# A decode step's output in two column halves, with filler products on TensorE

## The chip, the cores and the metric

The kernel runs on one core of a Trainium2 chip. The core has TensorE (matrix products, PE in the profile), VectorE (DVE), ScalarE (ACT), GpSimd (POOL) and SyncE (SP); SP and ACT issue the transfers here, and 16 transfer engines carry them out. The metric is the time of one execution on the device in microseconds (us), as the median of several runs.

## The reference

One decode step for two sequences (B = 2, one token each, D = 448): layernorm, attention of 16 query heads on 8 cached key and value heads (head size 256), limited to the last 2048 of 8192 cached positions, an output projection, and a gate from a small two-layer branch.

```python
W = min(4096, max(256, Sk // 4))                      # 2048
q = (xn @ wq)                                         # 2 x 16 heads x 256
scores = einsum(q, k[:, :, Sk - W:]) * Dh ** -0.5
o = softmax(scores) @ v[:, :, Sk - W:]
s = o.reshape(B, 1, 4096) @ wo                        # 2 x 448
g = silu(relu(xn @ w1) @ w2)                          # 2 x 448
return x + s * g                                      # bfloat16
```

All inputs are bfloat16. The keys and values inside the window are 2 x 16.8 MB; with the weights the kernel reads 44 MB and writes 1.8 KB.

## The kernel before

Every instruction is recorded by hand into one list for each engine (`pr.op`, `pr.dma`) with what it depends on; each engine runs its list in the order written, and waits on semaphores only where a dependence was given. There is no scheduler: the order of the Python code is the order on each engine. All products are recorded by the helper `mm`, so in the profile they all have its line (L246) and are told apart by their tiles.

The work goes in four units `u` (two sequences by two groups of four key heads). Each unit has one large buffer `kv[u]` of 128 partitions: first it holds K, later V. SP's queue carries nearly all the loads in this order: wq, w1, w2, K0 to K3, then V0, V1, V2 and the two halves of V3 (each V waits until the scores of its unit are done, as it overwrites K), then wo in six pieces of 16, 4, 4, 4, 2 and 2 rows a partition (`WO_PARTS`). ACT's queue loads x twice, as `x_sb` (two rows, for the layernorm) and as `x_c` (spread out for the last addition).

The order around the change:

- `do_H`, `do_F`: the gate's branch, early on. `do_F` brings the sum of four partial results to the layout of the output with a small float32 selection matrix (`bsel`), and makes silu with ACT's exponential and three VectorE steps, giving `g_sb`.
- For each unit: VectorE turns K (`do_turn`), TensorE makes scores (`do_S`), VectorE and ACT the softmax (`do_max`, `do_et`), and after the last one its results are spread into the weights `pt` (`do_spread`, `do_pt`).
- `do_PV(u)`: 32 products of 512 columns, in four column tiles of TensorE that run side by side, into the bank `obk`. For the last unit the second 16 wait for the second half of V3 (`d_vb`). `do_out(u)`: two VectorE steps take the result to `o_sb` (the buffer `xg`). `do_turn_out(hg)`: eight products and a VectorE copy (L368) turn it into `at2`, the weights of the output projection.
- The output projection: for the first 16 rows of wo (`WO_TILED`) 16 products of 448 columns into `wbk`, four side by side, copied by VectorE to `wc` (L448). The other 16 rows go straight into `fbk` (`direct`): for each row four products of 112 columns, one in each column tile, so that a quarter of the output's columns comes out in each group of 32 partitions. `at2` has 32 columns a row of wo, of which columns 0 and 16 hold the two sequences and the others zeros. Between rows 19 and 20 `wc` is added into `fbk` with `bsel`.
- The end: `fbk` times `g_sb` (L468), plus `x_c` (L470), over 128 partitions of 112 columns; then two stores, one for each sequence: SP stores the first, ACT the second, each as four rows of 112 values that lie 32 partitions apart.

Of the kernel before, what the change touches and what calls it, by code (L numbers as in the profile page):

```python
# [74 lines left out]
def bass_recurrent_scan__sliding_block_cached__dense_activation_relu__decode_kernel(  # L75
# [11 lines left out]
    B, Sq, D = A_x.shape  # L87
    _, HKV, SK, DH = A_k_cache.shape
# [10 lines left out]
    SLOTS = 7  # L99
    HC = HD // 2  # L100
    FC = DFF // 2
    NCOL = D // 4
    WO_PARTS = [16, 4, 4, 4, 2, 2]
    WO_TILED = 16

    es = contextlib.ExitStack()
    with es:
        pr = _Prog(nc, es)

        def named(name, shape, dt):  # L110
            return es.enter_context(nc.sbuf_tensor(name, shape, dt))
# [17 lines left out]
        bsel = named("bsel", [128, 32], F32)  # L129
# [45 lines left out]
        def rows(t):  # L175
            w = t.shape[1]
            return bass.AP(t, 0, [[16 * w, 8], [1, w]])

        def kv_src(u, cache):
            b, hg = divmod(u, 2)  # L180
            return cache[b, 4 * hg:4 * hg + 4, SK - W:SK, :].rearrange("g (p t) d -> p g (t d)", t=NT)

        d_x = pr.dma(ACTE, x_sb[0:B, :], A_x[:, 0, :])
        p_xc = pr.op(POOL, lambda e: e.memset(x_c[:, :], 0.0))
        d_xc = pr.dma(ACTE, rows(x_c), A_x.rearrange("b s (i n) -> i (b s) n", i=4), [p_xc])
        wq_src = A_wq.rearrange("r (hf c) -> (r hf) c", hf=2).rearrange("(p s) c -> p (s c)", s=SLOTS)
        w1_src = B_w1.rearrange("r (hf c) -> (r hf) c", hf=2).rearrange("(p s) c -> p (s c)", s=SLOTS)
        w2_src = B_w2.rearrange("(p j) n -> p (j n)", j=14)
# [7 lines left out]
        for u in range(NU):  # L196
# [4 lines left out]
            out=ident[:, :], in_=ident[:, :], compare_op=ALU.not_equal, fill=1.0,  # L201
            base=0, pattern=[[-1, 128]], channel_multiplier=1), [i0])
        p_z = [pr.op(POOL, lambda e, t=t: e.memset(t[:, :], 0.0))
               for t in (asel, bsel, rm, bt, qstat, at2)][-1]

        v_bn = pr.op(DVE, lambda e: e.bn_stats(st6[0:B, :], x_sb[0:B, :]), [d_x])
        v_ag = pr.op(DVE, lambda e: e.bn_aggr(st2[0:B, :], st6[0:B, :]), [v_bn])
# [7 lines left out]
        def z(t):  # L215
            return a_z[t.name]
# [17 lines left out]
        v_bs = pr.op(DVE, lambda e: e.tensor_copy(view(bsel, 0, [[16, 2]]), f8[:, 0:2]), [v_f8, p_z])  # L234
# [10 lines left out]
        def mm(out_ap, lhsT, rhs, start, stop=False, **kw):  # L245
            return lambda e: e.matmul(out_ap, lhsT=lhsT, rhs=rhs, start=start, stop=stop,  # L246
                                      skip_group_check=True, **kw)
# [83 lines left out]
        def do_rs():  # L331
# [2 lines left out]
                out=view(rs, 0, [[2, NU], [1, 2]]), in0=view(half2, 0, [[0, NU], [1, 2]]),  # L334
                in1=view(rinv, 0, [[1, NU], [0, 2]]), op=ALU.mult), [v, v_h2])

        def do_PV(u):
            bank, p, v = obk, pt[u], kv[u]
            deps = [d_v[u], st["pt", u], z(bank), st.get(("osb", u - 1))]
            for n in range(NT // 2):  # L340
                i = n % 4
                if u == NU - 1 and n == NT // 4:
                    deps = [d_vb]
                o = pr.op(PE, mm(bank[32 * i:32 * i + 16, :], p[:, 16 * n:16 * n + 16],
                                 v[:, 2 * n * DH:2 * n * DH + 2 * DH],
                                 n < 4, n >= NT // 2 - 4, tile_position=(0, 32 * i)), deps)
                deps = []
            last_PV[u] = o
# [9 lines left out]
                op0=ALU.mult, op1=ALU.add), [v])  # L358

        def do_turn_out(hg):  # L360
            deps = [st["osb", 2 + hg], v_as, st["mbk"]]
            lo = 64 * hg
            for dq in range(8):
                o = pr.op(PE, mm(mbk[lo:lo + 64, 288:352], asel[:, 7 - dq:71 - dq],
                                 view(o_sb, hg * 2 * DH + 32 * dq, [[DH, B], [1, 32]]),
                                 dq == 0, dq == 7, tile_position=(0, lo)), deps)
                deps = []
            st["at"] = st["mbk"] = pr.op(DVE, lambda e: e.tensor_copy(  # L368
                view(at2, 0, [[16, B], [32, 32]], n=64, p0=lo), view(mbk, 288, [[32, B], [1, 32]], n=64, p0=lo)), [o, p_z])

        def do_H():
            deps = [st["w1"], v_xr, v_q]
# [12 lines left out]
        def do_F():  # L385
            deps = [st["w2"], st["h"], z(fbk)]
            for j in range(14):
                i = j % 4
                o = pr.op(PE, mm(fbk[32 * i:32 * i + B, 0:D], h_sb[:, 32 * j:32 * j + 2], w2_sb[:, j * D:j * D + D],
                                 j < 4, j >= 10, tile_position=(0, 32 * i)), deps)  # L390
                deps = []
            v = pr.op(DVE, lambda e: e.tensor_copy(zc[:, :], fbk[:, 0:D]), [o])
            deps = [v, v_bs, st["mbk"]]
# [4 lines left out]
            a_e = pr.op(ACTE, lambda e: e.activation(ea[:, :], mbk[:, 128:128 + NCOL], ACT.Exp, scale=-1.0), [o])  # L398
            v = pr.op(DVE, lambda e: e.tensor_scalar(
                out=ea[:, :], in0=ea[:, :], scalar1=1.0, scalar2=None, op0=ALU.add), [a_e])  # L400
            v = pr.op(DVE, lambda e: e.reciprocal(tmp[:, :], ea[:, :]), [v])
            st["g"] = st["mbk"] = pr.op(DVE, lambda e: e.tensor_tensor(
                out=g_sb[:, :], in0=mbk[:, 128:128 + NCOL], in1=tmp[:, :], op=ALU.mult), [v])
# [35 lines left out]
        for n in WO_PARTS:  # L439
            landed[j0] = pr.dma(SP, wqo[:, j0 * D:(j0 + n) * D], wo_src[:, j0 * D:(j0 + n) * D], [m_q])  # L440
            j0 += n
        deps = [st["at"], z(wbk)]
        for j in range(WO_TILED):
            i = j % 4
            o = pr.op(PE, mm(wbk[32 * i:32 * i + B, 0:D], view(at2, 32 * j, [[16, 2]]), wqo[:, j * D:j * D + D],
                             j < 4, j >= WO_TILED - 4, tile_position=(0, 32 * i)), deps + [landed.get(j)])
            deps = []
        v_wc = pr.op(DVE, lambda e: e.tensor_copy(wc[:, :], wbk[:, 0:D]), [o])  # L448
# [19 lines left out]
        v_t = pr.op(DVE, lambda e: e.tensor_tensor(  # L468
            out=tmp[:, :], in0=fbk[:, 0:NCOL], in1=g_sb[:, :], op=ALU.mult), [m_o, st["g"]])
        v_o = pr.op(DVE, lambda e: e.tensor_tensor(  # L470
            out=out_sb[:, :], in0=tmp[:, :], in1=x_c[:, :], op=ALU.add), [v_t, d_xc])
# [34 lines left out]
```

## Time and profile before

| | |
|---|---|
| median of 3 runs | 111.02 us (110.95 to 111.13) |
| the profiled execution | 110.76 us, of which the span from the first to the last instruction is 109.4 us |
| busy, share of the span | PE 51%, DVE 56%, ACT 8%, POOL 3% |
| read from memory | 44.11 MB, 403 GB/s over the span |
| chain that ended last, by engine | DMA 57%, DVE 28%, PE 7%, SP's queue 5% |
| mean granted TensorE clock | 0.875 |

A row of a timeline or of the groups names line, engine, operation, output tile and input tiles, shape and count; in square brackets or behind the last bar stands how long the engine was idle before it and what ended that. A share of the granted clock of 1.00 is TensorE's full speed, 0.50 half of it. In the row of a stretch each engine has its busy time and, in parentheses, its instructions.

### The profile page before, as it was taken

Reading aid. Unit: us, or ns where it says so; the run is one execution under the profiler, and the core shown is the slowest. Engines: PE = TensorE matmul, PEld = TensorE weight load, DVE = VectorE, ACT = ScalarE, POOL = GpSimd, SP = SyncE. Lnnn points to the kernel's source line nnn. Section 1 sums busy time; section 2 is a strip of 40 time slices with the busy share of each in tenths; the row PEclk is TensorE's granted clock in tenths of the full one; section 3 lists DMA queues with packets and bytes.
Section 4 is the critical chain, followed back from the end, with each engine's and each line's share of the span. In section 5 each row is a group of like instructions: output and inputs, shape, how many; then the busy total and the mean of one; then the engine's idle time right before and its main releaser. Section 6 shows DMA issues by size and latency. Waiting matters only on the chain.

```text
span 109.4 us, 1124 instructions
## 1 busy us (share of the span) xinstructions
PE 55.5 (51%) x479; PEld 15.0 (14%) x479; DVE 61.6 (56%) x84; ACT 9.0 (8%) x18; POOL 2.9 (3%) x13
## 2 busy tenths in 40 slices
PE   0010649450000079929943994499349555425780
PEld 0000204110000011001200120111033122201350
DVE  2920046424099979999999999920457333103122
ACT  2970000000000000002000200020110000000000
POOL 7300000000000000000000000000000000000000
PEclk9999999999999999985996799589955899955559
DMA  6898999999999989998999899999999999999940
GB/s 158 356 472 365 426 436 494 395 479 449 395 395 479 467 383 395 491 455 383 407 494 431 383 419 503 419 395 413 503 407 395 413 431 431 425 421 405 400 170 1
DMA packets 2628, 44.17 MB, mean 404 GB/s; under 512 B 318, under 2 KB 576, under 8 KB 960
## 3 DMA queue, kind: packets, MB, share of 16 engines
q1 hardware_dynamic: 2600, 44.11, 94.6%
q8 instruction: 3, 0.05, 0.2%
q10 hardware_dynamic: 24, 0.00, 0.0%
q14 instruction: 1, 0.01, 0.0%
HBM read 44.11 MB, written 0.00 MB: 403 GB/s over the span
## 4 chain that ended last, share of the span: by engine, by line
DMA 57%; DVE 28%; PE 7%; SPq 5%; issue 1%
DMA kv<-in_A_k_cache_dram 34%; DVE kv L281 24%; DMA wqo<-in_A_wo_dram 23%; PE sbk L246 7%; SPq L35 5%; DVE q_x L310 1%; DVE rm L298 1%; DVE rm_t L300 0%; DVE bias L304 0%; DVE bt L301 0%; PE fbk L246 0%; DVE tmp L468 0%; DVE out_sb L470 0%
## 5 line engine op out<-in xcount | busy, mean ns | idle before, releaser
L246 PE MATMUL sbk<-kv,qstat 128*8 128x512 bf16 x128 | 30.0, 1085 | 23.3 <-DVE kv L281 23.3
L281 DVE STREAM_TRANSPOSE kv<-kv 128x2048 f32<-128x2048 f32 x16 | 35.6, 2274 | 4.9 <-DMA kv<-in_A_k_cache_dram 4.9
L246 PE MATMUL obk<-kv,pt 128*16 128x512 bf16 x128 | 10.3, 472 | 6.3 <-DMA kv<-in_A_v_cache_dram 3.6
L246 PEld LDWEIGHTS sbk<-kv,qstat 128*8 128x8 bf16 x128 | 4.8, 107 | 47.1 <-DVE kv L281 29.5
L353 DVE TENSOR_SCALAR o_odd<-obk,rs 128x256 f32<-128x256 f32 x4 | 1.9, 484 | 11.9 <-PE obk L246 11.9
L305 ACT ACTIVATE e_sb<-sbk,bias 128x512 bf16<-128x512 f32 x4 | 2.8, 689 | 52.1 <-DVE bias L304 52.1
L246 PE MATMUL qbk<-wqo,xr 128*4 128x512 bf16 x28 | 3.2, 626 | 5.4 <-DMA wqo<-in_A_wq_dram 5.4
L264 DVE TENSOR_SCALAR q_x<-qbk 128x512 bf16<-128x512 f32 x1 | 0.7, 691 | 8.4 <-PE qbk L246 8.4
L298 DVE TENSOR_REDUCE rm<-sbk 128x1 f32<-128x512 f32 x4 | 2.6, 662 | 4.8 <-PE sbk L246 4.8
L246 PEld LDWEIGHTS obk<-kv,pt 128*16 128x16 bf16 x128 | 3.4, 101 | 12.0 <-issue 6.4
L310 DVE STREAM_TRANSPOSE q_x<-e_sb 128x512 bf16<-128x512 bf16 x4 | 2.8, 690 | 1.7 <-ACT e_sb L305 1.7
L246 PE MATMUL mbk<-ident,xg 2*128 2x2 bf16 x7 | 0.3, 163 | 6.1 <-DVE xg L239 6.1
L327 DVE TENSOR_TENSOR pt<-spk,pmask 128x512 bf16<-128x512 f32 x4 | 2.6, 683 | 0.8 <-PE spk L246 0.8
L246 PE MATMUL qbk<-w_sb,xr 128*2 128x448 bf16 x28 | 2.8, 572 | 0.0
L246 PE MATMUL fbk<-w_sb,h_sb 128*2 128x448 bf16 x14 | 1.7, 566 | 1.5 <-issue 1.5
L246 PE MATMUL fbk<-wqo,at 128*32 128x112 bf16 x64 | 2.1, 287 | 0.2 <-DMA wqo<-in_A_wo_dram 0.2
L246 PE MATMUL spk<-q_x,perm 128*32 128x128 bf16 x16 | 0.6, 296 | 3.1 <-DVE q_x L310 3.1
L246 PE MATMUL mbk<-xg,asel 128*64 128x64 bf16 x16 | 1.1, 221 | 2.2 <-DVE xg L356 2.2
L275 DVE CAST qstat<-mbk 32x256 bf16<-32x256 f32 x4 | 1.7, 421 | 0.7 <-PE mbk L246 0.7
L246 PE MATMUL wbk<-wqo,at 128*2 128x448 bf16 x16 | 1.7, 567 | 0.7 <-DMA wqo<-in_A_wo_dram 0.7
L356 DVE SCALAR_TENSOR_TENSOR xg<-obk,rs,o_odd 128x256 bf16<-128x256 f32 x4 | 1.9, 484 | 0.1
L246 PEld LDWEIGHTS fbk<-wqo,at 128*32 128x32 bf16 x64 | 1.6, 133 | 1.0 <-DMA wqo<-in_A_wo_dram 0.8
(70 smaller groups left out, 31.9 us busy)
## 6 DMA issues: line engine op xcount, KB each, us to landing
kv<-in_A_k_cache_dram SPq DMA_DIRECT2D x4, 4096.0 KB, 41.2
kv<-in_A_v_cache_dram SPq DMA_DIRECT2D x3, 4096.0 KB, 22.1
kv<-in_A_v_cache_dram SPq DMA_DIRECT2D x2, 2048.0 KB, 17.6
wqo<-in_A_wq_dram SPq DMA_DIRECT2D x1, 3584.0 KB, 11.1
w_sb<-in_B_w_dram SPq DMA_DIRECT2D x2, 1568.0 KB, 16.0
wqo<-in_A_wo_dram SPq DMA_DIRECT2D x1, 1792.0 KB, 23.4
wqo<-in_A_wo_dram SPq DMA_DIRECT2D x3, 448.0 KB, 24.4
wqo<-in_A_wo_dram SPq DMA_DIRECT2D x2, 224.0 KB, 25.1
```

Of the source, the lines that this page charges most:

```text
L35: o = _Op(eng, lambda e: e.dma_start(dst, src), [d for d in deps if d is not None], True)
L246: return lambda e: e.matmul(out_ap, lhsT=lhsT, rhs=rhs, start=start, stop=stop, skip_group_check=True, **kw)
L264: v_q = pr.op(DVE, lambda e: e.tensor_scalar(out=view(q_x, 0, [[256, 8], [128, 2], [1, 32]]), in0=view(qbk, 0, [[64, 8], [1, 2], [2, 32]]) ...
L275: st["q"] = st["mbk"] = pr.op(DVE, lambda e, Q=Q: e.tensor_copy(qstat[32 * Q:32 * Q + 32, 256 * Q:256 * Q + 256], mbk[32 * Q:32 * Q + 32, ...
L281: st["turn", u] = pr.op(DVE, lambda e, n=n: e.transpose(kf[:, 2048 * n:2048 * n + 2048], kf[:, 2048 * n:2048 * n + 2048]), [d_k[u]])
L298: v = pr.op(DVE, lambda e: e.tensor_reduce(out=rm[:, 0:1], in_=sbk[u % 2][:, :], axis=AX.X, op=ALU.max), [last_S[u], p_z, st.get(("rmt", u ...
L305: st["exp", u] = pr.op(ACTE, lambda e: e.activation(e_sb[:, :], sbk[u % 2][:, :], ACT.Exp, bias=bias[:, 0:1], accum_out=ssum[:, u:u + 1]), ...
L310: st["et", u] = pr.op(DVE, lambda e: e.transpose(q_x[:, 512 * u:512 * u + 512], e_sb[:, :]), [st["exp", u], m_qt])
L327: st["pt", u] = pr.op(DVE, lambda e: e.tensor_tensor(out=view(pt[u], 0, [[8, 64], [2, 4], [1, 2]]), in0=view(spk, 128 * u, [[2, 64], [0, 4 ...
L353: v = pr.op(DVE, lambda e: e.tensor_scalar(out=o_odd[:, :], in0=obk[:, DH:2 * DH], scalar1=rs[:, 2 * u + 1:2 * u + 2], scalar2=None, op0=A ...
L356: st["osb", u] = pr.op(DVE, lambda e: e.scalar_tensor_tensor(out=o_sb[:, lo:lo + DH], in0=obk[:, 0:DH], scalar=rs[:, 2 * u:2 * u + 1], in1 ...
```

## The change

The output is laid out as two column halves of 224 in place of four quarters of 112 (`NCOL = D // 2`). Half `c` of both sequences lies in partitions 32c and 32c + 1. So `direct` and the additions with the float32 selection have two column tiles in place of four, with two weight columns in place of 32; `at2` shrinks to two columns a row of wo, `bsel` goes (the first two columns of `f8` do its work), and the element-wise steps of the gate and of the end run on 34 partitions (`ROWS`) of 224 columns. `x_c` is loaded by two transfers. At the end SP stores the first column half of both sequences and ACT the second, each as two rows of 224 values from two adjacent partitions.

Besides, `fill(n)` records n products that nobody reads: 32 weight columns of the identity times 512 columns of `kv[0]`, into the first bank of the scores. What they depend on is long done. There are 19: ten before the second half of the last `do_PV`, two before the last `do_turn_out`, four before the first product of wo, one before the addition of `wc`, one each before rows 20 and 24.

```diff
-    NCOL = D // 4
+    NCOL = D // 2
+    ROWS = 34
...
-        at2 = named("at2", [128, 32 * 32], BF)
+        at2 = named("at2", [128, 32 * 2], BF)
...
-        d_xc = pr.dma(ACTE, rows(x_c), A_x.rearrange("b s (i n) -> i (b s) n", i=4), [p_xc])
+        d_xc = [pr.dma(ACTE, x_c[32 * c:32 * c + B, :], A_x[:, 0, NCOL * c:NCOL * c + NCOL], [p_xc]) for c in range(2)]
...
+        def fill(n):
+            for _ in range(n):
+                pr.op(PE, mm(sbk[0][0:32, :], ident[:, 0:32], kv[0][:, 0:512], True, True), [st["exp", 2], d_v[0]])
+
         def do_PV(u):
...
                 if u == NU - 1 and n == NT // 4:
+                    fill(10)
                     deps = [d_vb]
...
         def do_turn_out(hg):
+            if hg:
+                fill(2)
...
-            for i in range(4):
-                o = pr.op(PE, mm(mbk[32 * i:32 * i + 32, 128:128 + NCOL], bsel[:, :],
-                                 zc[:, NCOL * i:NCOL * i + NCOL], True, True, tile_position=(0, 32 * i)), deps)
+            for c in range(2):
+                o = pr.op(PE, mm(mbk[32 * c:32 * c + B, 0:NCOL], f8[:, 0:B], zc[:, NCOL * c:NCOL * c + NCOL],
+                                 True, True, tile_position=(0, 32 * c)), deps)
...
+        fill(4)
         deps = [st["at"], z(wbk)]
...
         def direct(j, deps):
-            for i in range(4):
-                lo = j * D + i * NCOL
-                o = pr.op(PE, mm(fbk[32 * i:32 * i + 32, 0:NCOL], at2[:, 32 * j:32 * j + 32], wqo[:, lo:lo + NCOL],
-                                 j == WO_TILED, j == 31, tile_position=(0, 32 * i)), deps)
+            for c in range(2):
+                lo = j * D + c * NCOL
+                o = pr.op(PE, mm(fbk[32 * c:32 * c + B, 0:NCOL], at2[:, B * j:B * j + B], wqo[:, lo:lo + NCOL],
+                                 j == WO_TILED, j == 31, tile_position=(0, 32 * c)), deps)
...
         for j in range(WO_TILED, 20):
             direct(j, [landed.get(j), st["g"]])
+        fill(1)
         deps = [v_wc]
-        for i in range(4):
-            pr.op(PE, mm(fbk[32 * i:32 * i + 32, 0:NCOL], bsel[:, :], wc[:, NCOL * i:NCOL * i + NCOL], False,
-                         tile_position=(0, 32 * i)), deps)
+        for c in range(2):
+            pr.op(PE, mm(fbk[32 * c:32 * c + B, 0:NCOL], f8[:, 0:B], wc[:, NCOL * c:NCOL * c + NCOL], False,
+                         tile_position=(0, 32 * c)), deps)
...
         for j in range(20, 32):
+            if j in (20, 24):
+                fill(1)
             m_o = direct(j, [landed.get(j)])
...
-            out=tmp[:, :], in0=fbk[:, 0:NCOL], in1=g_sb[:, :], op=ALU.mult), [m_o, st["g"]])
+            out=tmp[0:ROWS, :], in0=fbk[0:ROWS, 0:NCOL], in1=g_sb[0:ROWS, :], op=ALU.mult), [m_o, st["g"]])
...
-        for b, eng in ((0, SP), (1, ACTE)):
-            d_o = pr.dma(eng, out[b].rearrange("s (i n) -> (s i) n", i=4),
-                         bass.AP(out_sb, 16 * b * NCOL, [[32 * NCOL, 4], [1, NCOL]]), [v_o])
+        for c, eng in ((0, SP), (1, ACTE)):
+            d_o = pr.dma(eng, out[:, 0, NCOL * c:NCOL * c + NCOL], out_sb[32 * c:32 * c + B, :], [v_o])
             pr.op(eng, None, [d_o])
```

More of the change, by code (lines that the diff above doesn't have):

```diff
@@ L203, in bass_recurrent_scan__sliding_block_cached__dense_activation_relu__decode_kernel @@
         p_z = [pr.op(POOL, lambda e, t=t: e.memset(t[:, :], 0.0))
-               for t in (asel, bsel, rm, bt, qstat, at2)][-1]
+               for t in (asel, rm, bt, qstat, at2)][-1]
         v_bn = pr.op(DVE, lambda e: e.bn_stats(st6[0:B, :], x_sb[0:B, :]), [d_x])
@@ L368, in do_turn_out @@
             st["at"] = st["mbk"] = pr.op(DVE, lambda e: e.tensor_copy(
-                view(at2, 0, [[16, B], [32, 32]], n=64, p0=lo), view(mbk, 288, [[32, B], [1, 32]], n=64, p0=lo)), [o, p_z])
+                view(at2, 0, [[1, B], [B, 32]], n=64, p0=lo), view(mbk, 288, [[32, B], [1, 32]], n=64, p0=lo)), [o, p_z])
         def do_H():
@@ L392, in do_F @@
             v = pr.op(DVE, lambda e: e.tensor_copy(zc[:, :], fbk[:, 0:D]), [o])
-            deps = [v, v_bs, st["mbk"]]
-            for i in range(4):
-                o = pr.op(PE, mm(mbk[32 * i:32 * i + 32, 128:128 + NCOL], bsel[:, :],
-                                 zc[:, NCOL * i:NCOL * i + NCOL], True, True, tile_position=(0, 32 * i)), deps)
+            deps = [v, v_f8, st["mbk"]]
+            for c in range(2):
+                o = pr.op(PE, mm(mbk[32 * c:32 * c + B, 0:NCOL], f8[:, 0:B], zc[:, NCOL * c:NCOL * c + NCOL],
+                                 True, True, tile_position=(0, 32 * c)), deps)
                 deps = []
-            a_e = pr.op(ACTE, lambda e: e.activation(ea[:, :], mbk[:, 128:128 + NCOL], ACT.Exp, scale=-1.0), [o])
+            a_e = pr.op(ACTE, lambda e: e.activation(ea[0:ROWS, :], mbk[0:ROWS, 0:NCOL], ACT.Exp, scale=-1.0), [o])
             v = pr.op(DVE, lambda e: e.tensor_scalar(
-                out=ea[:, :], in0=ea[:, :], scalar1=1.0, scalar2=None, op0=ALU.add), [a_e])
-            v = pr.op(DVE, lambda e: e.reciprocal(tmp[:, :], ea[:, :]), [v])
+                out=ea[0:ROWS, :], in0=ea[0:ROWS, :], scalar1=1.0, scalar2=None, op0=ALU.add), [a_e])
+            v = pr.op(DVE, lambda e: e.reciprocal(tmp[0:ROWS, :], ea[0:ROWS, :]), [v])
             st["g"] = st["mbk"] = pr.op(DVE, lambda e: e.tensor_tensor(
-                out=g_sb[:, :], in0=mbk[:, 128:128 + NCOL], in1=tmp[:, :], op=ALU.mult), [v])
+                out=g_sb[0:ROWS, :], in0=mbk[0:ROWS, 0:NCOL], in1=tmp[0:ROWS, :], op=ALU.mult), [v])
         def load_v(u, lo=0, hi=NT):
@@ L444, in bass_recurrent_scan__sliding_block_cached__dense_activation_relu__decode_kernel @@
             i = j % 4
-            o = pr.op(PE, mm(wbk[32 * i:32 * i + B, 0:D], view(at2, 32 * j, [[16, 2]]), wqo[:, j * D:j * D + D],
+            o = pr.op(PE, mm(wbk[32 * i:32 * i + B, 0:D], at2[:, B * j:B * j + B], wqo[:, j * D:j * D + D],
                              j < 4, j >= WO_TILED - 4, tile_position=(0, 32 * i)), deps + [landed.get(j)])
@@ L459, in bass_recurrent_scan__sliding_block_cached__dense_activation_relu__decode_kernel @@
             direct(j, [landed.get(j), st["g"]])
+        fill(1)
         deps = [v_wc]
-        for i in range(4):
-            pr.op(PE, mm(fbk[32 * i:32 * i + 32, 0:NCOL], bsel[:, :], wc[:, NCOL * i:NCOL * i + NCOL], False,
-                         tile_position=(0, 32 * i)), deps)
+        for c in range(2):
+            pr.op(PE, mm(fbk[32 * c:32 * c + B, 0:NCOL], f8[:, 0:B], wc[:, NCOL * c:NCOL * c + NCOL], False,
+                         tile_position=(0, 32 * c)), deps)
             deps = []
         for j in range(20, 32):
+            if j in (20, 24):
+                fill(1)
             m_o = direct(j, [landed.get(j)])
         v_t = pr.op(DVE, lambda e: e.tensor_tensor(
-            out=tmp[:, :], in0=fbk[:, 0:NCOL], in1=g_sb[:, :], op=ALU.mult), [m_o, st["g"]])
+            out=tmp[0:ROWS, :], in0=fbk[0:ROWS, 0:NCOL], in1=g_sb[0:ROWS, :], op=ALU.mult), [m_o, st["g"]])
         v_o = pr.op(DVE, lambda e: e.tensor_tensor(
-            out=out_sb[:, :], in0=tmp[:, :], in1=x_c[:, :], op=ALU.add), [v_t, d_xc])
-        for b, eng in ((0, SP), (1, ACTE)):
-            d_o = pr.dma(eng, out[b].rearrange("s (i n) -> (s i) n", i=4),
-                         bass.AP(out_sb, 16 * b * NCOL, [[32 * NCOL, 4], [1, NCOL]]), [v_o])
+            out=out_sb[0:ROWS, :], in0=tmp[0:ROWS, :], in1=x_c[0:ROWS, :], op=ALU.add), [v_t] + d_xc)
+        for c, eng in ((0, SP), (1, ACTE)):
+            d_o = pr.dma(eng, out[:, 0, NCOL * c:NCOL * c + NCOL], out_sb[32 * c:32 * c + B, :], [v_o])
             pr.op(eng, None, [d_o])
```

5 lines of the change are left out of this document (removed).

## The prediction

> **What bounds the kernel now.** I read the page first (transfer rows and chain), then the chain's last steps, then the timeline of each engine over the last 16 us, then the same time in stretches that end where the granted clock steps.
>
> ```profile
> span 109.4 us, 1124 instructions
> ...
> DMA  6898999999999989998999899999999999999940
> ...
> DMA 57%; DVE 28%; PE 7%; SPq 5%; issue 1%
> ```
> ```profile
> 81.31 25.14 DMA wqo<-in_A_wo_dram
> 106.44 0.04 issue
> 106.48 0.31 PE fbk L246 x8
> ```
>
> The transfer engines are nine tenths busy in almost every slice, and the chain's last long piece is the queue itself: the last sixth of wo is issued at 81.31 and lands at 106.44 because everything ahead of it has to pass first. All that comes behind it is a short tail: 109.44 - 106.44 = 3.0 us. A change behind the loads can move only that tail, unless it makes TensorE late for the landing.
>
> ```profile
> 93.35 1.04 PE L246 MATMUL obk<-kv,pt 128*16 128x512 bf16 x16
> 97.94 1.89 PE L246 MATMUL obk<-kv,pt 128*16 128x512 bf16 x16 [3.55 <-DMA kv<-in_A_v_cache_dram]
> 100.94 0.64 PE L246 MATMUL mbk<-xg,asel 128*64 128x64 bf16 x8 [1.11 <-DVE xg L356]
> 102.28 1.67 PE L246 MATMUL wbk<-wqo,at 128*2 128x448 bf16 x16 [0.70 <-DMA wqo<-in_A_wo_dram]
> 103.72 0.59 PE L246 MATMUL fbk<-wqo,at 128*32 128x112 bf16 x16
> 104.67 0.60 PE L246 MATMUL fbk<-wc,bsel 128*32 128x112 f32 x8 [0.35 <-DVE wc L448]
> 105.04 1.27 PE L246 MATMUL fbk<-wqo,at 128*32 128x112 bf16 x40
> 106.48 0.28 PE L246 MATMUL fbk<-wqo,at 128*32 128x112 bf16 x8 [0.17 <-DMA wqo<-in_A_wo_dram]
> ```
> ```profile
> 101.61 0.44 DVE L368 CAST at<-mbk 64x64 bf16<-64x64 f32 x1 [0.73 <-PE mbk L246]
> 103.99 0.62 DVE L448 COPY wc<-wbk 128x448 f32<-128x448 f32 x1 [1.94 <-PE wbk L246]
> 106.82 0.28 DVE L468 TENSOR_TENSOR tmp<-fbk,g_sb 128x112 f32<-128x112 f32 x1 [2.20 <-PE fbk L246]
> 107.13 0.28 DVE L470 TENSOR_TENSOR out_sb<-tmp,x_c 128x112 bf16<-128x112 f32 x1
> ```
> ```profile
> 107.43 0.66 SPq L35 DMA_DIRECT2D out_dram<-out_sb  x1
> 107.43 0.55 ACTq L35 DMA_DIRECT2D out_dram<-out_sb  x1
> ```
>
> The tail is 0.3 us of products, 0.6 us of two VectorE steps, and 109.44 - 107.43 = 2.0 us for the two stores. TensorE was ready only 0.17 us before the last rows of wo, so in this execution it has almost no slack to lose. And it was slow: the two halves of the last PV are the same 16 products, 1.04 us and 1.89 us. The stretches say why.
>
> ```profile
> 85.71:89.12 3.41, 1.90 (x32) 0.77 (x32) 1.27 (x3) 0.00 (x0) 0.00 (x0) 1.00 0.89 380
> 89.12:92.53 3.41, 1.90 (x32) 0.77 (x32) 1.24 (x4) 0.00 (x0) 0.00 (x0) 1.00 1.01 432
> 92.53:95.95 3.42, 1.41 (x24) 0.64 (x24) 0.82 (x2) 0.00 (x0) 0.00 (x0) 1.00 1.00 421
> 95.95:99.36 3.41, 1.42 (x16) 0.41 (x16) 0.00 (x0) 0.00 (x0) 0.00 (x0) 0.50 1.01 433
> 99.36:102.77 3.41, 1.60 (x24) 0.78 (x20) 1.41 (x3) 0.00 (x0) 0.00 (x0) 0.50 0.96 395
> 102.77:106.19 3.42, 3.06 (x80) 1.86 (x68) 0.62 (x1) 0.00 (x0) 0.00 (x0) 0.50 0.70 277
> ```
>
> Columns: busy us of PE, weight loads, DVE, ACT, POOL, then granted clock, transfer share, GB/s. Stretches with 1.90 us of PE work are followed by clock 1.00; the one with 1.41 is followed by 0.50, which lasts until the stretch with 3.06 is over. So the wait for the second half of V3 (3.55 us) halves the clock for nearly all of the output projection.
>
> [...]
>
> **The change part by part.**
>
> Price of a product: eight rounds of four 512-column products take 1.90 us at full clock, four rounds 1.04, so a round is (1.90 - 1.04) / 4 = 0.215 us and the rest (0.18) is filling and draining. At half clock four rounds take 1.89, hence about 0.43 a round. A filler is one 512-column product alone: 0.215 or 0.43 us.
>
> *Ten fillers behind the first half of V3.* TensorE stands from 94.39 (93.35 + 1.04) to 97.94. Clock there is full until 95.95, and with fillers the stretch 92.53 to 95.95 holds about 1.41 + 1.5 = 2.9 us of work, so it stays full: 10 x 0.215 = 2.15, done at 96.6. Price 0, covered by 1.4 us of waiting that is left; at half clock they would take 4.3 and end 0.7 late. PV's second half then takes 1.04, ending 98.98.
>
> *Two fillers before the last turn of o* run to 99.4 under the two VectorE steps (98.98 to about 100.0): price 0. The turn takes about 0.44 in place of 0.64.
>
> *Four fillers before wo's first 16 rows:* from 100.45 to 101.3. The copy that feeds the rows is done at 100.0 + 0.44 + 0.03 + 0.44, 100.9, but the rows themselves land only near 102.24 (the 0.70 us wait above ends there), so price 0 with 0.9 us left.
>
> *wbk* then takes 1.04 x 448/512, about 0.93 (before 1.67), ending 103.2; wc is copied by 103.9. *Direct products* have two column tiles of 224 in place of four of 112: per row twice the time at one clock, 224/512 x 0.215 = 0.094, against 0.047. Rows 16 to 19 need 0.4, the filler 0.2, the float32 product of wc doubles in length but runs at twice the clock (0.60 less drain, again about 0.4). Rows 20 to 27 need 0.75 and two fillers 0.43. From 103.9 this sums to 105.5 to 105.6, and rows 28 and 29 follow their landing. TensorE is ready for the last landing with some 0.3 us to spare. Price of fillers and half the column tiles together: 0 so long as the clock is full.
>
> *The last two rows* (behind the landing): the second begins 0.094 after the first in place of 0.07 at least, and the last product streams 0.047 longer: +0.07 us, on the path.
>
> *The two last VectorE steps* now have 34 rows of 224. Length, not rows, sets the price:
>
> ```profile
> L327 DVE TENSOR_TENSOR pt<-spk,pmask 128x512 bf16<-128x512 f32 x4 | 2.6, 683 | 0.8 <-PE spk L246 0.8
> ...
> L332 DVE RECIPROCAL rinv<-mbk 128x4 f32<-128x4 f32 x1 | 0.2, 171 | 0.0
> ```
>
> (683 - 275)/400 = 1.02 ns an element, so 275 + 114 = 389 ns each, +0.23 us for both, on the path. x_c now has two semaphores; the second wait lies beside the first step.
>
> *The stores.* Two rows of 448 B each in place of four of 224. No such store is in the trace; the nearest row is the two-row load of x at the start, on ACT's queue:
>
> ```profile
> 0.74 0.55 ACTq L35 DMA_DIRECT2D x_sb<-in_A_x_dram  x1
> ...
> 2.07 0.62 DVE L206 BATCH_NORM_STATS2 st<-x_sb 2x6 f32<-2x448 bf16 x1 [2.07 <-DMA x_sb<-in_A_x_dram]
> ...
> 11.86 3.16 PE L246 MATMUL qbk<-wqo,xr 128*4 128x512 bf16 x28 [5.43 <-DMA wqo<-in_A_wq_dram]
> ```
>
> Its user starts 1.33 us after its issue; the pair of four-row stores takes 2.0. So the gain lies between 0 and 0.65. A loss is excluded: those rows of 896 B were longer than the new ones. I take two thirds, 0.43: the row count is that of the load, but the stores still come as a pair from two engines, and SP's half took 0.66 to issue against 0.55.
>
> [...]
>
> *The start.* x_c becomes two loads: one more issue on ACT (0.55), behind it ACT's table load, square root and clears. TensorE waits 5.43 us for wq there, so nothing comes of it. Without that cover it would cost 0.55. The bsel memset and its copy go, and POOL's clearing of at2 shrinks: off the path.
>
> *Gate of the second branch* (exp, add, reciprocal, product on 224 columns):
>
> ```profile
> 24.77 0.85 DVE L401 RECIPROCAL tmp<-ea 128x112 f32<-128x112 f32 x1
> 25.66 0.27 DVE L402 TENSOR_TENSOR g_sb<-mbk,tmp 128x112 f32<-128x112 f32 x1
> 30.03 8.89 DVE L281 STREAM_TRANSPOSE kv<-kv 128x2048 f32<-128x2048 f32 x4 [4.10 <-DMA kv<-in_A_k_cache_dram]
> ```
>
> The reciprocal costs (853 - 171)/108 = 6.3 ns an element, +0.71; with the other steps and the longer products under 1.6 us, hidden by VectorE's 4.10 us wait for K. Uncovered it would be 1.6.
>
> **Sum:** +0.07 + 0.23 - 0.43 = -0.13 us. The profiled execution took 110.76, 0.26 below the median 111.02; the forecast goes from the median: 110.9.
>
> **The rivals.**
>
> *The stores don't get shorter.* For it: of the 2.0 us, 1.3 lie behind SP's 0.66 of issuing, and nothing shows that rows set them. Against: 1.33 in all for two rows. Then +0.07 + 0.23 = +0.30, 111.3, slower. [...]
>
> *The clock halves all the same.* Place: the stretch 99.36 to 102.77. With the change it holds the turn 0.44, four fillers 0.86 and wbk's first 0.5, 1.8 us: between 1.41 (followed by half) and 1.90 (followed by full), nearer the latter. If work in one column tile counts for less, or the steps lie elsewhere, the fillers turn against the kernel. At half clock throughout the projection: the turn ends 100.6, four fillers 102.4, wbk 103.9 (streaming), rows 16 to 19 104.6, filler 105.05, wc 105.8, filler 106.2; then, full clock again, rows 20 to 31 and one filler, 12 x 0.094 + 0.215 = 1.35, and drain 0.2: 107.8 against 106.77 before. That is +1.0 for TensorE, with the tail's +0.23 - 0.43 about +0.8: 111.8. It decides once TensorE reaches row 30 after 106.48. [...]
>
> *The fillers do nothing that matters.* TensorE waits for the last landing anyway, at either clock; then they only pay for the halved column tiles. This is part of the likeliest case. Where an execution before the change had half clock at its last eight products, a further 0.1 is gained: 110.8 or less.
>
> **How the numbers follow.** Likeliest (0.60): full clock, store gain 0.25 to 0.65, so 110.67 to 111.07, centre 110.9. A further gain of 0.1 or more: 0.08, about 110.75. Stores unchanged: 0.15, 111.3. Half clock: 0.17, about 111.8. The range 110.55 to 111.5 leaves out the half-clock case and little else. One 0.2% (0.22 us) is about what a measurement of this kernel can tell; below 110.80 lie some 0.25 of the likeliest case and the 0.08, together about 0.34; above 111.24 the two bad cases, 0.30 with a part of the stores' case within the bound; the rest, 0.36, within.
>
> **What would show it.** Right: granted clock 1.00 from 95.95 to the end of the products; the wait for V3's second half still there, about 1.4 us; the last landing still near 106.44 and TensorE waiting for it; the last two VectorE steps 0.39 each; from the issue of the stores to the end 1.5 to 1.6. Wrong: clock 0.50 around 103 and no wait for the last rows of wo; a store phase of 2.0 again; or a last landing that moved, which nothing here accounts for.

## The result and the profile after

The changed kernel takes 110.67 us (median of 7 runs, 110.53 to 110.87), the kernel before on the same chip 111.13 us (7 runs, 110.95 to 111.24). The ratio is 0.9963, 95% interval 0.995 to 0.9976: 0.41 us faster, with 0.27 to 0.56 us in the interval (by the medians 0.46). The forecast was 110.9 us, 0.13 us faster. The profiled execution of the changed kernel took 110.67 us, its span 109.3 us.

The end of the chain of waits of the changed kernel (start, length, what; us):

```profile
81.24 25.50 DMA wqo<-in_A_wo_dram
106.75 0.04 issue
106.79 0.38 PE fbk L241 x4
107.17 0.02 issue
107.19 0.40 DVE tmp L474
107.58 0.02 issue
107.61 0.38 DVE out_sb L476
```

TensorE's and then the two store engines' part of its timeline (rows left out are marked; `sbk<-kv,ident` are the fillers):

```profile
93.35 1.04 PE L241 MATMUL obk<-kv,pt 128*16 128x512 bf16 x16 [0.17 <-DMA kv<-in_A_v_cache_dram]
94.21 2.32 PE L241 MATMUL sbk<-kv,ident 128*32 128x512 bf16 x10
98.22 1.04 PE L241 MATMUL obk<-kv,pt 128*16 128x512 bf16 x16 [1.68 <-DMA kv<-in_A_v_cache_dram]
...
102.53 0.93 PE L241 MATMUL wbk<-wqo,at 128*2 128x448 bf16 x16 [0.76 <-DMA wqo<-in_A_wo_dram]
...
106.79 0.35 PE L241 MATMUL fbk<-wqo,at 128*2 128x224 bf16 x4 [0.21 <-DMA wqo<-in_A_wo_dram]
...
108.02 0.33 SPq L35 DMA_DIRECT2D out_dram<-out_sb  x1
108.02 0.26 ACTq L35 DMA_DIRECT2D out_dram<-out_sb  x1
```

And stretches of 3.41 us (columns as in the prediction). In the traces before and after, the granted clock held for 3.41 us or a multiple of it between two steps, 3.41 to 23.89; in this one it was full from 85.07 to 108.96:

```profile
95.30:98.71 3.41, 1.73 (x18) 0.65 (x20) 0.00 (x0) 0.00 (x0) 0.00 (x0) 1.00 1.01 426
98.71:102.13 3.42, 2.38 (x26) 0.87 (x18) 1.20 (x3) 0.00 (x0) 0.00 (x0) 1.00 0.96 399
102.13:105.54 3.41, 2.95 (x39) 1.38 (x39) 0.62 (x1) 0.00 (x0) 0.00 (x0) 1.00 0.87 344
```

The loads still set the end: TensorE waits 0.21 us for the last rows. In this execution these landed at 106.75, 0.31 later than in the one profiled before, so the two profiles differ by less than the medians (the execution profiled before was 0.26 us under its median, the one after is its median). What the change does is in the tail behind the landing: 109.35 - 106.75 = 2.6 us in place of 3.0 (109.35 is the span to two places, 109.349 in the trace). Its parts, after against before: the last products 0.38 against 0.31; the two VectorE steps with the gaps up to the stores 108.02 - 107.19 = 0.83 against 107.43 - 106.82 = 0.61; the stores, from issue to the end, 109.35 - 108.02 = 1.33 against 2.01. That is +0.07 + 0.22 - 0.68 = -0.39 us. The stores are also issued in half the time, 0.33 and 0.26 us against 0.66 and 0.55. With the fillers the clock is full through all of the projection in this execution, and both halves of the last PV take 1.04 us.

### The profile page after: what moved, and what is told of

The parts are those of the page before. It is cut to its first block, busy times and chain, and to the rows that moved or that the text cites. A ratio compares the mean times of both kernels' runs of the same rounds, so it can differ in the third digit from the quotient of the medians.

```text
span 109.3 us, 1081 instructions
## 1 busy us (share of the span) xinstructions
PE 57.0 (52%) x458; PEld 14.5 (13%) x458; DVE 62.2 (57%) x83; ACT 9.1 (8%) x18; POOL 2.1 (2%) x12
## 4 chain that ended last, share of the span: by engine, by line
DMA 57%; DVE 28%; PE 7%; SPq 5%; issue 1%
DMA kv<-in_A_k_cache_dram 34%; DVE kv L276 24%; DMA wqo<-in_A_wo_dram 23%; PE sbk L241 7%; SPq L35 5%; DVE q_x L305 1%; DVE rm L293 1%; DVE rm_t L295 0%; DVE bias L299 0%; DVE bt L296 0%; DVE tmp L474 0%; DVE out_sb L476 0%; PE fbk L241 0%
## 5 line engine op out<-in xcount | busy, mean ns | idle before, releaser
L241 PE MATMUL obk<-kv,pt 128*16 128x512 bf16 x128 | 9.3, 435 | 4.8 <-DVE xg L356 2.4
L241 PEld LDWEIGHTS sbk<-kv,qstat 128*8 128x8 bf16 x128 | 4.0, 107 | 48.4 <-DVE kv L276 30.2
L241 PE MATMUL sbk<-kv,ident 128*32 128x512 bf16 x19 | 5.1, 380 | 0.0
L241 PE MATMUL fbk<-wqo,at 128*2 128x224 bf16 x32 | 2.5, 258 | 0.4 <-DMA wqo<-in_A_wo_dram 0.4
L451 DVE COPY wc<-wbk 128x448 f32<-128x448 f32 x1 | 0.6, 625 | 2.4 <-PE wbk L241 2.4
L241 PEld LDWEIGHTS sbk<-kv,ident 128*32 128x32 bf16 x19 | 1.8, 97 | 1.8
```

## The experiments

Theory A at the start: the gain is the shorter store, short because a store has two rows in place of four; the fillers only pay for the halved column tiles. Rivals: the gain is TensorE's full clock; or the place of the rows makes the store short, not their number. The runs of a group had one chip and shared the runs of the kernel before; differences are given against these.

### Without the fillers

```diff
         def fill(n):
-            for _ in range(n):
+            for _ in range(0):
```

> The changed kernel without its 19 fillers. Theory A (the gain is the shorter store, the fillers only pay for the halved column tiles): the granted clock falls to 0.50 from about 96 to 106 us, TensorE reaches the last rows of wo 0.3 to 0.8 us late, and the gain of 0.4 us is gone: -0.1 to +0.4 us against the kernel before. Rival (TensorE waits for the last landing at either clock, the fillers do nothing): -0.4 us as with them.

Measured: 111.16 us (10 runs, 110.36 to 111.78) against 111.26; ratio 0.9969, interval 0.9934 to 1.0004. The gain is no longer clear of the noise: 0.10 us by the medians, 0.34 by the ratio, with a gain of 0.73 and a loss of 0.04 as the bounds. That interval holds the changed kernel's gain of 0.41 too, so the run does not decide between theory A and the rival. The times lie over a band of 1.4 us, where the changed kernel's first seven lay within 0.34. The execution profiled was the quickest: the clock fell to half in the wait for V3 and stepped up near 104.7 (the products of rows 16 to 19, from 103.74, took 0.96 us, as in the run at half clock below with 0.95; those of wc, from 104.68, took 0.55, against 0.91 there), and TensorE waited 0.18 us for the last rows. The two stretches around the fall:

```profile
91.09:94.50 3.41, 1.68 (x28) 0.64 (x24) 1.19 (x3) 0.00 (x0) 0.00 (x0) 1.00 1.04 447
94.50:97.91 3.41, 0.00 (x0) 0.00 (x0) 0.00 (x0) 0.00 (x0) 0.00 (x0) 0.50 0.97 407
```

One more execution of the same kernel was profiled, on the same chip:

> The changed kernel without fillers once more, one look, since its ten times lay between 110.36 and 111.78 us and only one of the fastest was profiled. If its slow executions are late products at half clock: clock 0.50 until after the last rows of wo have landed, TensorE busy across the landing, and a time of 111.1 us or more; where the clock steps up before the landing, 110.4 to 110.8 us as in the first look.

It took 110.80 us. Its stretches and the end of its chain:

```profile
96.24:99.65 3.41, 1.61 (x16) 0.41 (x16) 0.00 (x0) 0.00 (x0) 0.00 (x0) 0.50 0.99 419
99.65:103.06 3.41, 1.61 (x20) 0.77 (x20) 1.20 (x3) 0.00 (x0) 0.00 (x0) 0.50 0.96 396
103.06:106.48 3.42, 3.42 (x36) 1.62 (x30) 0.62 (x1) 0.00 (x0) 0.00 (x0) 0.50 0.64 251
```
```profile
79.11 23.12 DMA wqo<-in_A_wo_dram
102.23 0.14 issue
102.37 1.66 PE wbk L241 x16
104.03 3.26 PE fbk L241 x36
```

Here the clock is half until 106.48, and the chain leaves the loads at 102.23, with the first piece of wo; from there it runs through TensorE alone to 107.3. TensorE no longer waits for the last rows: it is late by 0.2 to 0.35 us. That is an estimate: in six other profiles (before, after, without fillers, fillers alone, rows 16 and 32 apart) the products of the last piece of wo started 4.20 to 4.32 us after those of the first, which from 102.37 gives 106.57 to 106.69, and with 0.38 for the products an end at 106.95 to 107.07; measured was 107.30. In these two executions, with two column tiles and no fillers, the step up came near 104.7 and at 106.48, and only the later one made TensorE late. The time, 110.80, is what was expected where the clock steps up before the landing (110.4 to 110.8), although TensorE was busy across it. The slowest executions (111.5 to 111.8) were not profiled; that their clock stayed low longer is an inference, and the mean clocks on record (0.78 to 0.86 in the three slowest, 0.80 to 0.89 in the four quickest) do not settle it.

### The fillers alone

```diff
+        def fill(n):
+            for _ in range(n):
+                pr.op(PE, mm(sbk[0][0:32, :], ident[:, 0:32], kv[0][:, 0:512], True, True), [st["exp", 2], d_v[0]])
...
                 if u == NU - 1 and n == NT // 4:
+                    fill(10)
```

(the other five calls of `fill` as in the change; the rest is the kernel before)

> The kernel before with the same 19 fillers at the same places and nothing else. Theory A: clock 1.00 to the end, TensorE waits longer for the last rows, and the time moves by 0 to -0.1 us. Rival (the full clock is what the change gains): -0.3 to -0.5 us.

Measured: 111.06 us (10 runs, 110.94 to 111.31) against 111.26; ratio 0.9983, interval 0.9969 to 0.9997. That is -0.2 us, between what theory A allowed (-0.1) and the rival (-0.3); the interval, -0.34 to -0.03, reaches into both. The band is narrow here too (0.4 us, against 110.83 to 112.41 for the kernel before). That the kernel before had executions in which the half clock cost something is an inference from this; the one profiled, with a step up at 106.19, just ahead of the last landing (106.44), was not one of them. Two later runs with the same four column tiles and no fillers show such executions (adjacent partitions alone, then pairs of adjacent rows). In both the last eight products took 0.41 us in place of 0.31, as at half clock (sixteen such products took 0.59 us at 0.50 in the profile before, 0.38 with the fillers):

```profile
106.61 0.41 PE fbk L246 x7
...
106.88 0.41 PE fbk L246 x8
```

That would be 0.1 of the 0.2 us; the rest stays open.

### Two rows a store, but not adjacent ones

```diff
-        for b, eng in ((0, SP), (1, ACTE)):
-            d_o = pr.dma(eng, out[b].rearrange("s (i n) -> (s i) n", i=4),
-                         bass.AP(out_sb, 16 * b * NCOL, [[32 * NCOL, 4], [1, NCOL]]), [v_o])
...
+        for i, eng in ((0, SP), (2, ACTE), (1, SP), (3, ACTE)):
+            d_o.append((eng, pr.dma(eng, out[:, 0, NCOL * i:NCOL * i + NCOL],
+                                    bass.AP(out_sb, 32 * i * NCOL, [[16 * NCOL, 2], [1, NCOL]]), [v_o])))
```

> The kernel before with its eight output rows in four stores of two rows, two behind each other on each of SP and ACT. If the number of rows in one store sets its length: the first two are over 1.33 us after their issue, the others start about 0.3 us later, so 1.6 to 1.7 us from the first issue to the end in place of 2.0, -0.3 us. Rival (the number of rows in all, or their adjacency, sets it): 2.0 us or more, 0 to +0.3 us.

Measured: 112.07 us (5 runs) against 111.26, ratio 1.0068, interval 1.0044 to 1.0093: 0.8 us slower, more than either side expected.

And in the changed kernel:

```diff
-        for c, eng in ((0, SP), (1, ACTE)):
-            d_o = pr.dma(eng, out[:, 0, NCOL * c:NCOL * c + NCOL], out_sb[32 * c:32 * c + B, :], [v_o])
+        for b, eng in ((0, SP), (1, ACTE)):
+            d_o = pr.dma(eng, out[b].rearrange("s (c n) -> (s c) n", c=2),
+                         bass.AP(out_sb, b * NCOL, [[32 * NCOL, 2], [1, NCOL]]), [v_o])
```

> The changed kernel with one sequence in each store: two rows of 224 that lie 32 partitions apart, next to each other in memory. If the number of rows sets the length: 1.33 us from issue to end, the time of the changed kernel (-0.4 us against before) within 0.1. Rival (it is the adjacent partitions that gain): 1.6 to 2.0 us, -0.1 to +0.3 us.

Measured: 111.23 us (10 runs) against 111.26, ratio 0.9993, interval 0.9976 to 1.0009. The gain is gone. The head and the stores of the two timelines, rows 16 apart first, then rows 32 apart:

```profile
core 0 of [0], span 110.5 us
...
107.79 1.48 SPq L35 DMA_DIRECT2D out_dram<-out_sb  x2
107.79 1.24 ACTq L35 DMA_DIRECT2D out_dram<-out_sb  x2
```
```profile
core 0 of [0], span 109.8 us
...
107.90 0.63 SPq L35 DMA_DIRECT2D out_dram<-out_sb  x1
107.90 0.56 ACTq L35 DMA_DIRECT2D out_dram<-out_sb  x1
```

The two-row stores from partitions 16 apart take 0.74 and 0.62 us each to issue (half of the two rows above), and 2.7 us from the first issue to the end of all four; those from 32 apart 0.63 and 0.56 to issue and 1.9 to the end. Theory A's reason falls: two rows that lie apart are hardly shorter than four (2.0). That leaves theory B: what shortens the store is that its rows lie in adjacent partitions.

### Adjacent partitions alone

```diff
-                         bass.AP(out_sb, 16 * b * NCOL, [[32 * NCOL, 4], [1, NCOL]]), [v_o])
+                         bass.AP(out_sb, 32 * b * NCOL, [[NCOL, 4], [1, NCOL]]), [v_o])
```

> The kernel before, its two stores of four rows of 112 values reading four adjacent partitions in place of four that lie 32 apart; nothing else is different (the rows stored are then the wrong ones: the output's values are left out of this run). Theory B, from the runs with rows 16 and 32 partitions apart (adjacency sets the length, not the number of rows): issue about 0.3 us and 1.3 to 1.45 us from issue to end, -0.5 to -0.65 us against before. Rival (two rows and adjacency are both needed): 1.6 to 2.0 us, 0 to -0.4 us.

Measured: 110.44 us (5 runs, 110.27 to 111.04) against 111.20; ratio 0.9943, interval 0.9892 to 0.9994.

```profile
core 0 of [0], span 109.0 us
...
107.65 0.35 SPq L35 DMA_DIRECT2D out_dram<-out_sb  x1
107.65 0.28 ACTq L35 DMA_DIRECT2D out_dram<-out_sb  x1
```

Four rows of 224 B as before, in quarter-width columns and with no filler: issued in 0.35 and 0.28 us, over in 1.4 us. Theory B holds: with the partitions alone changed, the store is 0.6 us shorter, and four adjacent rows take hardly longer than two (1.33). Distances between 1 and 16 partitions were not tried, and why the distance counts no run shows. In the same group the changed kernel itself had

> The changed kernel as it is, on the same chip as the three beside it: -0.3 to -0.55 us against the kernel before, 1.3 us from the issue of the stores to the end. No theory says otherwise; it is the yardstick of this group.

Measured: 110.74 us (10 runs, 110.33 to 111.58) against 111.20; ratio 0.9956, interval 0.992 to 0.9992. The medians put the adjacent four-row stores 0.3 us ahead of it, about what its VectorE steps and last products cost (0.22 + 0.07); the intervals overlap. Its ten times lie over 1.25 us here, nearly as wide as without fillers on the other chip, where the kernel with its rows apart, fillers and all, lay within 0.31: a narrow band doesn't always come with the fillers.

### Fillers that start at half clock

```diff
                 if u == NU - 1 and n == NT // 4:
-                    fill(10)
                     deps = [d_vb]
```

> The changed kernel without the ten fillers behind the first half of V3, the nine later ones kept. The clock falls to half in the wait for V3 and the nine run at half clock. If the half-clock rival of the prediction is priced right, TensorE reaches the last rows up to 1.0 us late: +0.3 to +0.8 us against the changed kernel, in the worst phases of the clock steps +1.0. If fillers at half clock raise the clock soon enough: within 0.2 us of the changed kernel.

Measured: 110.78 us (10 runs, 110.42 to 111.14) against 111.20; ratio 0.996, interval 0.9937 to 0.9983: as the changed kernel, and not the 0.3 to 0.8 us more that the prediction's price would have made.

```profile
94.82:98.24 3.42, 0.00 (x0) 0.00 (x0) 0.00 (x0) 0.00 (x0) 0.00 (x0) 0.50 0.98 414
98.24:101.65 3.41, 2.87 (x21) 0.86 (x22) 0.97 (x2) 0.00 (x0) 0.00 (x0) 0.50 0.99 418
101.65:105.06 3.41, 3.39 (x46) 1.88 (x47) 0.86 (x2) 0.00 (x0) 0.00 (x0) 1.00 0.99 396
```

The clock does fall to 0.50 in the wait for V3. But PV's second half and the later fillers then fill their stretch (2.87 us of 3.41), and the clock is full again from 101.65, before the products of wo's first rows start (102.71). In these runs ten of the nineteen fillers are not needed.

### Four adjacent rows of 112 columns

```diff
-    NCOL = D // 2
-    ROWS = 34
+    NCOL = D // 4
+    HALF = D // 2
+    ROWS = 36
...
+        def four(t, c):
+            return bass.AP(t, 32 * c * NCOL, [[NCOL, 4], [1, NCOL]])
+
+        def pair(dram, c):
+            return dram[:, 0, HALF * c:HALF * c + HALF].rearrange("b (q n) -> b q n", q=2)
...
+            for q in range(2):
+                for c in range(2):
+                    lo = j * D + HALF * c + NCOL * q
+                    o = pr.op(PE, mm(fbk[32 * c:32 * c + 4, 0:NCOL], at2[:, 5 * j + 1 - q:5 * j + 5 - q],
+                                     wqo[:, lo:lo + NCOL], j == WO_TILED and q == 0, j == 31 and q == 1,
                                     tile_position=(0, 32 * c)), deps)
...
+            d_o = pr.dma(eng, pair(out, c), four(out_sb, c), [v_o])
```

> The changed kernel with both: two column tiles, but four adjacent partitions of 112 columns in each (weights padded with zero columns put each quarter of the columns in its own partition), so that the last two VectorE steps have 112 columns again and the stores four adjacent rows of 224 B. By theory B the stores stay at 1.3 to 1.45 us, VectorE gives back 0.22: -0.1 to -0.25 us against the changed kernel. Rival (four rows are slower than two whatever their place): stores 1.6 to 2.0, +0.1 to +0.45 us against the changed kernel.

Measured: 111.93 us (4 runs) against 111.20, ratio 1.0076, interval 1.0053 to 1.0098. That is 1.2 us over the changed kernel, more than even the rival allowed.

```profile
core 0 of [0], span 110.8 us
...
108.73 0.77 SPq L35 DMA_DIRECT2D out_dram<-out_sb  x1
108.73 0.66 ACTq L35 DMA_DIRECT2D out_dram<-out_sb  x1
```

The VectorE steps were short again (0.27 us), but the stores took 0.77 and 0.66 us to issue and 2.1 to the end: adjacent rows in the core's memory are not enough when the other side has two steps (two sequences by two quarters). Its two loads of x_c, with the same two steps, agree: 1.37 us to issue, where the changed kernel's two took 0.54. The last rows of wo landed only at 107.69; of this more below.

### Pairs of adjacent rows, two stores a queue

```diff
-                view(at2, 0, [[16, B], [32, 32]], n=64, p0=lo), view(mbk, 288, [[32, B], [1, 32]], n=64, p0=lo)), [o, p_z])
+                view(at2, 0, [[1, B], [32, 32]], n=64, p0=lo), view(mbk, 288, [[32, B], [1, 32]], n=64, p0=lo)), [o, p_z])
...
+        for i, eng in ((0, SP), (2, ACTE), (1, SP), (3, ACTE)):
+            d_o.append((eng, pr.dma(eng, out[:, 0, NCOL * i:NCOL * i + NCOL], out_sb[32 * i:32 * i + B, :], [v_o])))
```

> The kernel before with its four quarters of 112 columns and no fillers, the two sequences in adjacent partitions (32i and 32i + 1), and four stores of two adjacent rows, two behind each other on each of SP and ACT. By theory B (adjacent partitions issue in about 0.3 us) the second pair starts 0.33 us later, 1.65 to 1.75 us from the first issue to the end against 2.0: -0.2 to -0.35 us against before. Rival (a second store in a queue costs its full length whatever its rows, as in the run with rows 16 apart): +0.3 to +0.8 us.

Measured: 110.93 us (10 runs, 110.75 to 111.33) against 111.17; ratio 0.998, interval 0.9961 to 0.9999.

```profile
core 0 of [0], span 109.6 us
...
107.92 0.64 SPq L35 DMA_DIRECT2D out_dram<-out_sb  x2
107.92 0.56 ACTq L35 DMA_DIRECT2D out_dram<-out_sb  x2
```

Two adjacent-row stores behind each other are issued in the time of one with rows apart, and end 1.7 us after the first issue, as theory B had it. This is about half of the change's gain in the store, without its wider VectorE steps and without fillers: it is worth 0.2 us (0.01 to 0.43 in the interval).

### A bfloat16 product, at two places

```diff
+        tmp_b = named("tmp_b", [128, NCOL], BF)
         out_sb = named("out_sb", [128, NCOL], BF)
...
-            out=tmp[0:ROWS, :], in0=fbk[0:ROWS, 0:NCOL], in1=g_sb[0:ROWS, :], op=ALU.mult), [m_o, st["g"]])
+            out=tmp_b[0:ROWS, :], in0=fbk[0:ROWS, 0:NCOL], in1=g_sb[0:ROWS, :], op=ALU.mult), [m_o, st["g"]])
```

> The changed kernel with the product of the output and the gate written as bfloat16 in place of float32, so that the last VectorE step reads two bfloat16 tiles. If such a step is faster than the 383 ns of the float32 one: 0.2 to 0.3 us, -0.05 to -0.15 us against the changed kernel (-0.5 to -0.6 us against before). Rival: 383 ns as before, no difference.

Measured: 111.07 us (10 runs, 110.99 to 111.60) against 111.17; ratio 0.9999, interval 0.9979 to 1.002: no gain, where -0.5 to -0.6 us was expected. The same with the new tile's line moved behind that of the large buffers `kv`:

> The run with the bfloat16 product once more, same instructions, with the new tile declared behind the large buffers in place of ahead of them, so that these lie where they lie in the changed kernel (at a multiple of 128 B in each partition; in the run before they lay 64 B beside one). If that shift made its last landing late (107.24 us against 106.45 to 106.87 in the runs with multiples of 128): landing at 106.4 to 106.9, the last VectorE step 0.27 us, -0.45 to -0.65 us against before, 0.1 better than the changed kernel. Rival (chance, or the bfloat16 tile itself): landing past 107 again and the time within 0.1 us of before.

Measured: 110.60 us (6 runs, 110.33 to 110.68) against 111.16; ratio 0.9948, interval 0.9933 to 0.9963. The ends of the two chains:

```profile
81.70 25.54 DMA wqo<-in_A_wo_dram
107.24 0.04 issue
...
108.10 0.27 DVE out_sb L477
```
```profile
81.40 25.12 DMA wqo<-in_A_wo_dram
106.52 0.04 issue
...
107.38 0.27 DVE out_sb L477
```

The last step is 0.27 us in place of 0.38 in both. In the first the last rows land 0.72 us later, with the same instructions: what differs is the place of the buffers declared behind the tile, and the chip, on which the kernel before took the same time (111.17 and 111.16). The second of these profiles is the quickest execution of its kernel; against the kernel before the two medians differ by 0.46 us (-0.10 and -0.56). With the tile at the end this has the lowest median of the kernels that store the output's own rows: 0.56 us ahead of the kernel before, by the medians about 0.1 us ahead of the changed one, which is within the intervals.

## Why the prediction was right or wrong

*The landing bounds, only the tail moves:* right. In the profile after the chain still runs through the last piece of wo (the sixth of six pieces, two rows of 32), and the difference lies in the tail. The landing itself was 0.31 us later there, which the prediction names as a sign of being wrong. But in the twelve profiles whose large buffers lie at one place or 256 B from it (see the last section) it lay anywhere from 106.44 to 106.87, and 106.44, the one that the prediction had, is the earliest; the change isn't shown to move it.

*Last products +0.07, VectorE +0.23:* right; 0.07 and 0.22 measured.

*The store, -0.43:* mis-sized, and for a wrong reason. It measured -0.68, just past the upper end of the bounds (0.65). This term is nearly the whole of the gap between the forecast (-0.13) and the tail that was measured (-0.39). The row chosen, the two-row load of x, gave the right length, 1.33 us, in part by luck: 0.55 of it was issue, where the store's issue took 0.33. I read it as a matter of two rows and left a third of the gain out for the pair. The runs show that the partitions' distance sets the length: two rows 32 apart took 1.9 us, four adjacent ones 1.4. The load of x has two rows in adjacent partitions, and the trace of before could not tell the two properties apart.

*The rival of the unchanged store, 111.3:* it didn't come. With one store on each queue the pair took 1.33 to 2.1 us by its shape (1.33 with two adjacent rows, 2.01 with four that lie 32 partitions apart, 2.1 with two steps on the memory's side).

*Ten, two, four and three fillers, price 0:* right for each place in the profile after. The ten ended 1.68 us before V3's second half, the clock stayed full, TensorE waited 0.21 us at the last landing where 0.3 was forecast. The margin was thin: the stretch 95.30 to 98.71, with 1.73 us of work, was followed by full clock, one of 1.68 without fillers by half. In the run with four rows of 112 columns the ten took 3.69 us in place of 2.32, so the clock seems to have fallen in spite of them, and PV's second half followed without a wait; TensorE still waited 0.86 us for the first rows of wo, so nothing came of it:

```profile
95.14 3.69 PE L250 MATMUL sbk<-kv,ident 128*32 128x512 bf16 x10
98.86 1.04 PE L250 MATMUL obk<-kv,pt 128*16 128x512 bf16 x16
...
103.29 0.93 PE L250 MATMUL wbk<-wqo,at 128*2 128x448 bf16 x16 [0.86 <-DMA wqo<-in_A_wo_dram]
```

*The fillers gain nothing:* not so in the kernel before, where they alone gave -0.2 us (-0.34 to -0.03). The forecast had 0.1 for executions whose last products ran at half clock, and only as a side case; two traces of kernels without fillers show such executions. One profiled execution, in which the step up came just in time, stood for all of them. Whether the fillers gain anything in the changed kernel, beyond paying for the halved column tiles, is not shown: the interval without them (-0.73 to +0.04 us) holds the gain with them. In the profiles here the clock's steps fall at other places from one execution to the next (the step up near 104.7 and at 106.48 without fillers, at 106.19 in the kernel before). The bands of the times don't show that it is the fillers that narrow them: 0.4 to 1.4 us in four runs without fillers, 0.3 to 0.4 in five with all of them, but 0.6 and 1.25 in two others. I had reckoned with other places of the steps mainly against the change.

*The half-clock rival, 111.8:* it didn't come. The stretch nearest to the one I feared (98.71 to 102.13) held 2.38 us of work in the profile after. In the run without the first ten, the clock was 0.50 when the later fillers began, it was 1.00 again from 101.65, before it mattered, and no loss shows. The price was also at odds with its own condition. In the rows of before, a stretch with 1.41 us of work is followed by 0.50, one with 3.06 by 1.00. So too little work from 99.36 to 102.77 could halve the clock from 102.77 on, but the price runs the last turn of o and the four fillers, ahead of that, at half clock too. And it let the clock stay half through a stretch that the fillers themselves fill (2.87 us in the run without the first ten, and full clock behind it).

*Start and gate* (one more load, 1.6 us more on VectorE): nothing of them is seen at the end of the profile after, as forecast.

*The sum.* The tail measured -0.39 us from the two profiles, of which the fillers are no part. That alone meets the change's -0.41 (0.27 to 0.56) and, in the second group, its -0.46 by the medians. The -0.2 of the fillers alone does not come on top of it. That the halved column tiles use it up would fit, but is not shown.

## What to carry to other kernels

A small store at the end is worth laying out so that its rows lie in adjacent partitions and each side is a single step: here the adjacent partitions alone made 1.4 us of 2.0, and four rows of 224 B took about as long as two of 448 B. Where products wait for a load near the end, look at the spread of the times, not only at one profile, since it may be of a lucky execution: fillers that keep TensorE's clock up were worth about 0.2 us in the kernel before (0.03 to 0.34), where its profile showed nothing to gain. And after an edit that adds or resizes a tile, look whether the large buffers behind it have moved: in the two runs where they had, other than by 256 B, the last rows landed at 107.24 and 107.69 us, in the others at 106.87 or earlier.

## What the runs showed that was not expected

*The issue time follows the partitions.* Stores with rows apart, or with two steps on the memory's side, took 0.54 to 0.77 us to issue; with adjacent rows and one step 0.25 to 0.35. The two loads of x_c in the changed kernel, adjacent partitions too, took 0.54 together, where the single one of eight rows 16 apart took 0.63. The load of x took 0.55 although its rows are adjacent; it is the first transfer on ACT's queue, and why it is slow stays open.

*The place of the large buffers.* By the declared sizes of the tiles ahead of them, two runs moved them, against the changed kernel, by other than a multiple of 128 B in each partition (64 and 84 B beside one), and there the last rows landed at 107.24 and 107.69 us. In the twelve others the buffers lie as in the changed kernel or 256 B from there, and the rows landed between 106.44 and 106.87. The two kernels with a bfloat16 product have the same instructions, and their times do not overlap (110.99 to 111.60 and 110.33 to 110.68), which speaks for the place: 0.72 us of landing between the two profiles, 0.46 us between the medians. They ran on different chips, and the other late run differs in more than the place. Whether the multiple of 128 B is what counts is not shown: no other distances were tried.
